# Small products inside an FFN stream: pair 5's outputs in two parts, pair 6's first products later, the last pair's outputs in two parts

## The chip, the cores and the metric

The kernel runs on one core of one Trainium2 chip. The time is device microseconds (us) of one execution; medians are over several executions. The span in a profile is of one execution, from its first to its last instruction, and is about 1.7 us shorter than the time of the same execution (337.6 against 335.9 us for the kernel before). A change counts as faster or slower when the 95% interval of the ratio of times is clear of 2%, as the same when it lies within 2%, and as unclear when it holds the 2% line.

## The reference, cut to what matters

```
scores = scale * q @ k^T                    # 8 batches, 8 heads, 576 positions, 64 per head
ret    = (scores * Dmat) @ v                # Dmat[i, j] = gamma_h ** (i - j) for i >= j, else 0
x      = ret as (4608 tokens, 512)
a, b   = x @ w_a, x @ w_b                   # 512 -> 1536 each
out    = (a * b) @ w_out                    # 1536 -> 512, fp32
```

The kernel computes the first half by blocks: 18 pairs of 128-token blocks, with a running state (a 64 x 64 sum of k^T v per head) carried from block to block. The FFN takes 512 tokens (two pairs) at a time, in two of the ten blocks 256.

## The kernel before

TensorE gets one long stream of FFN products (`pa`, `pb`, `po`; 512 columns each, 256 in `pa` and `pb` of the two short blocks). The small products of the pairs are put between them, in "stretches". A stretch takes one pair out (its outputs `o`) and another in (its `kv` and its scores `sc`):

```python
    def stretch(into, outof):
        flush()                                   # work left for VectorE and ScalarE
        ...
        if outof is not None:
            o = ps_o[0].tile([128, 2, HP, 2, 64], FP32, tag="o", name="o2")
            begun = Begun()
            from_states(outof, o, begun)          # 32 small matmuls: outputs from states
            kp = int(0 in (block_of(outof, 0), block_of(outof, 1)))
            nc.scalar.copy(fence, o[:, :, 0, kp, 0])      # the "fence"
        if into is not None:
            convert, convert_swapped = keyed(into, outof is None)   # 32: kv
            masked = matched(into)                                  # 32: scores
        if outof is not None:
            scaled = from_keys(outof, o, begun)   # 32: outputs from keys, onto the same o
            later.append(lambda: scaled(0))
            later.append(lambda: scaled(1))
        ...
```

Both halves of the outputs add into the same PSUM tile, from different quarters of the array. The fence, a tiny ScalarE copy that reads the tile, makes the second half wait until the first is written. With `kv` and `sc` between them that wait is hidden.

Where a stretch goes is set by a list of positions, counted in FFN units (one unit is a product of 512 columns). Block 2 (256 tokens) covers units 216 to 288, of which 264 to 288 are its `po`; block 3 begins at 288 and needs the outputs of pairs 4 and 5.

```python
    todo += [(170, stretch, (3, None)), (197, stretch, (4, 3)),
             (232, stretch, (5, 4)), (266, stretch, (6, 5)),
             (372, stretch, (7, 6)), (408, stretch, (8, 7))]
    ...                                           # later pairs; the last is (None, 17)
    casts = {3: 104, 4: 104.1, 5: 141, 6: 200, 7: 250, 8: 330}
    turns = {4: 104.2, 5: 145, 6: 210, 7: 338, 8: 345}
    loads = {7: 212, 8: 271, 9: 345.1, 10: 345.2}
```

`casts` are GpSimd's conversions of q, k (`qkb`) and of v with its decay (`vb`); `turns` are two DMA transposes of `qkb` per pair, giving `qkT`; `loads` bring in q, k, v. Transposes, loads and stores share one DMA queue, issued in order by SyncE (SP).

## Time and profile before

| | kernel before |
|---|---|
| time, median (lowest to highest) | 337.17 us (335.87 to 337.80, 4 runs) |
| span of the profiled run | 335.9 us |
| TensorE busy | 322.2 us, 96% (3611 matmul records of 3648) |
| TensorE idle in the stretch (6 in, 5 out) | 2.23 + 1.27 us |
| mean granted clock, whole span | 0.988 |

Of the 13.7 us in which TensorE is not busy, part lies at the start and the end of the program (the first and the last slice are at 8 and 6 tenths), and part is no idle time at all: this trace lacks 37 matmul records, and a lacking record reads as idle time ended by "issue" (often a bracket of 0.16 us). The rest is what a change of order can win. The prediction below shows the lines: read the busy rows first, then the row of the granted clock, then who waited for whom. In a timeline line the first number is the start, the second the length, and the bracket the idle time before it with what ended it.

### The profile page before, as it was taken

Reading aid. Unit: us, or ns where it says so; the run is one execution under the profiler, and the core shown is the slowest. Engines: PE = TensorE matmul, PEld = TensorE weight load, DVE = VectorE, ACT = ScalarE, POOL = GpSimd, SP = SyncE. Lnnn points to the kernel's source line nnn. Section 1 sums busy time; section 2 is a strip of 40 time slices with the busy share of each in tenths; the row PEclk is TensorE's granted clock in tenths of the full one; section 3 lists DMA queues with packets and bytes.
Section 4 is the critical chain, followed back from the end, with each engine's and each line's share of the span. In section 5 each row is a group of like instructions: output and inputs, shape, how many; then the busy total and the mean of one; then the engine's idle time right before and its main releaser. Section 6 shows DMA issues by size and latency. Waiting matters only on the chain.

```text
span 335.9 us, 8671 instructions
## 1 busy us (share of the span) xinstructions
PE 322.2 (96%) x3611; PEld 169.4 (50%) x3648; DVE 162.1 (48%) x290; ACT 129.2 (38%) x277; POOL 114.6 (34%) x146
## 2 busy tenths in 40 slices
PE   8999999999599998999999999999999999999996
PEld 4644457868444454545454545454445444444443
DVE  5744445666433366565356535653465346413321
ACT  7725743554243343252335233523332433213321
POOL 3960178721558276446033703470340000000000
PEclk9999999999779999999999999999999999999999
DMA  7999999999699997994499448964860320031013
GB/s 207 252 189 204 265 224 221 172 219 216 108 204 254 217 209 189 217 208 73 130 213 209 79 125 182 213 113 122 180 139 4 119 70 0 2 94 33 1 23 102
DMA packets 143175, 50.37 MB, mean 150 GB/s; under 512 B 124576, under 2 KB 138656, under 8 KB 143136
## 3 DMA queue, kind: packets, MB, share of 16 engines
q1 hardware_dynamic: 138384, 45.10, 65.0%
q0 software_dynamic: 4752, 4.72, 8.7%
q8 instruction: 28, 0.46, 0.6%
q14 instruction: 11, 0.09, 0.1%
HBM read 37.75 MB, written 9.44 MB: 140 GB/s over the span
## 4 chain that ended last, share of the span: by engine, by line
PE 93%; issue 2%; DMA 1%; DVE 1%; POOL 1%; ACT 1%; ACTq 0%; DVEq 0%; POOLq 0%
PE po L716 28%; PE pb L697 27%; PE pa L682 26%; PE w L740 2%; PE o L602 2%; PE o L589 1%; PE sc L563 1%; DMA qkT<-qkb 1%; PE kv L359 1%; PE kv L506 1%; PE tp L316 1%; PE sc L331 1%; POOL qkb L444 1%; PE o L409 1%; PE pa L664 0%
## 5 line engine op out<-in xcount | busy, mean ns | idle before, releaser
L702 DVE TENSOR_TENSOR hT<-ha,pb 128x512 bf16<-128x512 bf16 (+1 forms) x120 | 75.7, 633 | 103.3 <-PE pb L697 98.1
L697 PE MATMUL pb<-xT,wb_sb 128*128 128x512 bf16 (+1 forms) x473 | 111.5, 357 | 0.5
L690 ACT CAST ha<-pa 128x512 bf16<-128x512 f32 (+1 forms) x120 | 64.7, 542 | 119.6 <-PE pa L682 118.4
L682 PE MATMUL pa<-xT,wa_sb 128*128 128x512 bf16 (+1 forms) x459 | 108.4, 357 | 1.4 <-issue 1.0
L716 PE MATMUL po<-wo_sb,hT 128*128 128x512 bf16 (+1 forms) x430 | 96.6, 378 | 2.7 <-issue 2.5
L697 PEld LDWEIGHTS <-wb_sb 128*128 128x128 bf16 x480 | 46.8, 98 | 46.4 <-issue 0.3
L682 PEld LDWEIGHTS <-wa_sb 128*128 128x128 bf16 x474 | 45.5, 98 | 45.1 <-issue 0.2
L716 PEld LDWEIGHTS <-hT 128*128 128x128 bf16 x444 | 42.7, 99 | 49.0 <-issue 3.2
L440 POOL CAST qkb<-qf 64x1024 bf16<-64x1024 f32 x15 | 15.4, 1029 | 87.0 <-DMA qf<-in_q_dram 76.9
L445 POOL TENSOR_TENSOR vb<-vf,vs 128x1024 bf16<-128x1024 f32 x15 | 28.5, 1901 | 15.0 <-PE o L602 5.4
L725 ACT COPY osb<-po 128x512 f32<-128x512 f32 (+1 forms) x21 | 12.1, 575 | 53.0 <-PE po L716 50.0
L727 DVE COPY osb<-po 128x512 f32<-128x512 f32 (+1 forms) x16 | 10.8, 674 | 40.6 <-PE po L716 40.6
L526 DVE TENSOR_TENSOR sums<-kv,sums 128x256 f32<-128x256 f32 x46 | 19.5, 423 | 2.8 <-PE kv L506 0.8
L612 DVE TENSOR_TENSOR xT<-o,qs 128x512 bf16<-128x512 f32 x30 | 19.5, 682 | 2.8 <-PE o L602 2.8
L572 DVE TENSOR_TENSOR sT<-sc,mask 128x512 bf16<-128x512 f32 x30 | 19.5, 679 | 0.0
L444 POOL CAST qkb<-kf 64x512 bf16<-64x512 f32 x30 | 17.6, 614 | 0.9
L444 POOL CAST qkb<-qf 64x512 bf16<-64x512 f32 x30 | 17.6, 614 | 0.6
L440 POOL CAST qkb<-kf 64x1024 bf16<-64x1024 f32 x15 | 15.5, 1033 | 5.3 <-DMA kf<-in_k_dram 4.8
L530 ACT CAST states<-sums 64x512 bf16<-64x512 f32 x26 | 16.0, 617 | 0.3
L740 PE MATMUL w<-ones 128*128 128x256 bf16 (+1 forms) x36 | 8.6, 370 | 1.5 <-DVE ones L197 1.5
L299 POOL CAST qkb<-kf 128x512 bf16<-128x512 f32 x5 | 3.1, 614 | 19.0 <-DMA kf<-in_k_dram 19.0
L631 ACT COPY fence<-o 128x2 f32<-128x2 f32 x15 | 2.4, 160 | 16.6 <-PE o L589 16.6
(81 smaller groups left out, 161.7 us busy)
## 6 DMA issues: line engine op xcount, KB each, us to landing
qf<-in_q_dram SPq DMA_DIRECT2D x32, 256.0 KB, 4.2
kf<-in_k_dram SPq DMA_DIRECT2D x32, 256.0 KB, 4.8
vf<-in_v_dram SPq DMA_DIRECT2D x32, 256.0 KB, 5.2
out_dram<-osb SPq DMA_DIRECT2D x25, 256.0 KB, 2.2
out_dram<-osb SPq DMA_DIRECT2D x22, 128.0 KB, 2.5
wo_sb<-in_moe_w_out_dram POOLq DMA_DIRECT2D x3, 512.0 KB, 16.8
qf<-in_q_dram SPq DMA_DIRECT2D x8, 128.0 KB, 3.3
kf<-in_k_dram SPq DMA_DIRECT2D x8, 128.0 KB, 3.4
```

The costliest lines, as they stand in the source:

```text
L440: nc.gpsimd.tensor_copy(qkb[0:64, w], t[0:64])
L444: nc.gpsimd.tensor_copy(to[:, :, 1 - r], fro[:, :, r])
L445: nc.gpsimd.tensor_tensor(vb.rearrange("p (k h d) -> p k h d", k=2, h=H), vf.rearrange("p (k h d) -> p k h d", k=2, h=H), vs2[:, 2 if n in ...
L526: nc.vector.tensor_tensor(sums[:, i], own, prev, op=ALU.add)
L530: nc.scalar.copy(to(half(1 - r)), fro(half(r)))
L572: nc.vector.tensor_tensor(sT[:, on].rearrange("p c k s -> p (c k) s"), sc[:, on].rearrange("p c k s -> p (c k) s"), mask3.unsqueeze(1).to_ ...
L612: nc.vector.tensor_tensor(x_of(t0, 128).rearrange("p c (a s) -> p c a s", a=2), o[:, :, :, kp].rearrange("p a c s -> p c a s"), qs[:, :, s ...
L682: nc.tensor.matmul(pa[:, 0:n], wa_sb[:, c, fs], xT[:, c], start=(c == 0), stop=(c == NC - 1))
L690: nc.scalar.copy(ha[:, 0:n], pa[:, 0:n])
L697: nc.tensor.matmul(pb[:, 0:n], wb_sb[:, c, fs], xT[:, c], start=(c == 0), stop=(c == NC - 1))
L702: nc.vector.tensor_tensor(hT[:, F, 0:n], has[F][:, 0:n], pb[:, 0:n], op=ALU.mult)
L716: nc.tensor.matmul(po[:, 0:width], hT[:, F, u * 128:(u + 1) * 128], wo_sb[:, F, cols], start=(F == 0), stop=(F == NF - 1))
```

## The change

Its intent: pair 6 is not ready when pair 5's outputs are due, so take the two apart. Pair 5's outputs are issued in two parts with four FFN products between, which also cover the fence; pair 6's first products go into block 3; and its transposes go behind pair 7's loads in the DMA queue. The last pair's outputs are also issued in two parts.

```diff
+    def open_outputs(n):
+        o = ps_o[0].tile([128, 2, HP, 2, 64], FP32, tag="o", name="o2")
+        begun = Begun()
+        from_states(n, o, begun)
+        kp = int(0 in (block_of(n, 0), block_of(n, 1)))
+        nc.scalar.copy(fence, o[:, :, 0, kp, 0])
+        opened[n] = o, begun
+    def close_outputs(n):
+        scaled = from_keys(n, *opened.pop(n))
+        later.append(lambda: scaled(0))
+        later.append(lambda: scaled(1))
+    def open_alone(n):
+        flush()
+        open_outputs(n)
 ...                                       # stretch() now uses these
-             (232, stretch, (5, 4)), (266, stretch, (6, 5)),
+             (232, stretch, (5, 4)), (266, open_alone, (5,)),
+             (270, close_outputs, (5,)), (312, stretch, (6, None)),
 ...
-                 (starts[n] - 44, stretch,
-                  (n + 2 if n + 2 < NP else None, n + 1))]
+                 (starts[n] - 44, stretch, (n + 2, n + 1))
+                 if n + 2 < NP else
+                 (starts[n] - 44, open_alone, (n + 1,))]
+    todo += [(starts[NP - 2] - 40, close_outputs, (NP - 1,))]
 ...
-    turns = {4: 104.2, 5: 145, 6: 210, 7: 338, 8: 345}
+    turns = {4: 104.2, 5: 145, 6: 240, 7: 338, 8: 345}
```

More of the change, by code (lines that the diff above doesn't have):

```diff
@@ L618, in from_keys @@
         return scaled
+    opened = {}
+    def open_outputs(n):
[12 more added lines that the diff above has]
+        open_outputs(n)
     def stretch(into, outof):
@@ L625, in stretch @@
         if outof is not None:
-            o = ps_o[0].tile([128, 2, HP, 2, 64], FP32, tag="o", name="o2")
-            begun = Begun()
-            from_states(outof, o, begun)
-            kp = int(0 in (block_of(outof, 0), block_of(outof, 1)))
-            nc.scalar.copy(fence, o[:, :, 0, kp, 0])
-        if into is not None:
-            convert, convert_swapped = keyed(into, outof is None)
-            masked = matched(into)
-        if outof is not None:
-            scaled = from_keys(outof, o, begun)
-            later.append(lambda: scaled(0))
-            later.append(lambda: scaled(1))
-        if into is not None:
-            later.append(lambda: (convert(), masked(0)))
-            later.append(lambda: (convert_swapped(), masked(1)))
+            open_outputs(outof)
+        convert, convert_swapped = keyed(into, outof is None)
+        masked = matched(into)
+        if outof is not None:
+            close_outputs(outof)
+        later.append(lambda: (convert(), masked(0)))
+        later.append(lambda: (convert_swapped(), masked(1)))
     WCOLS = [3, 4, 5]
```

## The prediction

> **What bounds the kernel now.** I read the page from the top: busy shares, then slices, then the list of waits, then the chain and the TensorE timeline where the slices dip.
>
> ```profile
> PE 322.2 (96%) x3611; PEld 169.4 (50%) x3648; DVE 162.1 (48%) x290; ACT 129.2 (38%) x277; POOL 114.6 (34%) x146
> ...
> PE   8999999999599998999999999999999999999996
> ...
> PEclk9999999999779999999999999999999999999999
> DMA  7999999999699997994499448964860320031013
> ```
>
> TensorE (PE) is the bound nearly everywhere. So only two things can change the time: what TensorE executes, which the change leaves alone (the instruction orders of the two kernels have the same 7298 TensorE rows), and the places where it stands still or runs at a lower clock. A slice is 335.9/40 = 8.4 us. There is one bad place after the start: slice 11 (84.0 to 92.4 us) has PE at 5, and slices 11 and 12 have the granted clock at 7. The list of waits names it:
>
> ```profile
> ACT fence L631 <- PE o L589: 16.6, 15, 2.5
> ...
> PE kv L506 <- POOL vb L445: 2.2, 1, 2.2
> ...
> PE sc L563 <- DMA qkT<-qkb: 1.3, 1, 1.3
> ...
> PE o L602 <- ACT fence L631: 0.3, 1, 0.3
> ```
>
> Three waits of TensorE, each happening once. The first two lie in the stretch that is changed first (pair 6 in, pair 5 out), the third in the one changed last (pair 17 out alone). Timeline of TensorE (start, length, what, idle before it):
>
> ```profile
> 85.51 1.02 PE L716 MATMUL po<-wo_sb,hT 128*128 128x512 bf16 x3
> 86.46 0.44 PE L589 MATMUL o<-qkT,states 64*64 64x64 bf16 x32
> 89.14 0.64 PE L506 MATMUL kv<-vb,qkb 64*64 64x64 bf16 x32 [2.23 <-POOL vb L445]
> 91.05 0.64 PE L563 MATMUL sc<-qkT 64*64 64x64 bf16 x32 [1.27 <-DMA qkT<-qkb]
> 91.50 0.62 PE L602 MATMUL o<-sT,vb 64*64 64x64 bf16 x32
> 92.46 5.89 PE L716 MATMUL po<-wo_sb,hT 128*128 128x512 bf16 x19 [0.33 <-issue]
> ```
>
> The stretch issues four groups of 32 small matmuls: pair 5's outputs from states (L589), pair 6's kv and scores (L506, L563), pair 5's outputs from keys (L602). Pair 6 is not ready, and as the order is fixed, pair 5's second half and the FFN products behind it wait too. The FFN products after it run at half pace. Both show in the windows (start:end, length, busy of five engines, granted clock, DMA share, GB/s), the first line being an undisturbed stretch (5 in, 4 out):
>
> ```profile
> 76.50:77.80 1.30, 1.30 (x123) 1.20 (x121) 0.42 (x1) 0.27 (x2) 0.00 (x0) 1.00 1.29 274
> ...
> 86.40:92.50 6.10, 2.26 (x130) 1.97 (x131) 1.95 (x5) 0.16 (x1) 2.61 (x3) 0.71 0.86 134
> 92.40:98.40 6.00, 5.94 (x21) 2.38 (x20) 2.33 (x4) 2.55 (x6) 2.60 (x4) 0.72 1.05 200
> ```
>
> Why pair 6 is late: its q lands at 82.54 us (GpSimd's cast starts there), GpSimd needs until 87.12 for the q and k casts and 89.09 for vb, and the second DMA transpose, issued at 87.14, lands 3.87 us later, at 91.01. Nothing of that chain waits for TensorE.
>
> **What the Trainium skill says.** (1) "TensorE: Matmul & The Clock Gate", Part 1: the array has a half-rate and a full-rate clock, falls back after about 3.4 us of idleness and needs about as long to recover; 512-column products start 426.7 ns apart cold and 215.7 warm. The trace agrees: the first weight loads of L716 after the bubble start at 92.46, 92.89, 93.31, 93.74 (0.427 apart), and warm FFN groups of four take 0.86 (0.216 each). (2) "TensorEngine Tiling (Array Packing)", Tiling Modes, Key Properties: changing the tiling mode drains TensorE. The trace shows a small sum: the weight load of the first small group has 0.42 us of idle time each time, and the stretch as a whole costs more than its matmuls (below). (3) "DMA: Bandwidth & Descriptors", Queues, rings and completion order: on each DMA engine descriptors are consumed in ring order. That fits q, k, v of a pair landing in the order issued, and bears on a rival below.
>
> **The change, part by part.**
>
> Part 1, cost of the stretch now. The last FFN slot before it starts at 86.16 (85.51 plus three spacings of 0.216; one record of four is missing), so FFN would continue at 86.37. The first product after it has no record either; one cold spacing before 92.46 gives 92.03. Delay: 92.03 - 86.37 = 5.66 us. The 20 output products left in the block then need until 98.18 (next pa), 6.15 us against 20 x 0.216 = 4.31: 1.84 us for the cold clock. Sum 7.50 us beyond plain FFN work.
>
> Part 2, cost of the same 128 matmuls when all is ready. A clean stretch later: last po slot before it ends its spacing at 256.94, groups start at 257.04, 257.31, 257.57, 257.89, and FFN resumes at 258.30 (258.51 less one unrecorded product). That is 1.36 us: about 0.28 per group of 32, and 0.10 at entry plus some 0.13 at exit, so about 0.23 for one change of mode.
>
> Part 3, after. Pair 5's first half: 0.23 + 0.28 = 0.51. Four FFN products (no cost; they had to run anyway, and cover the fence, whose ACT copy takes 0.16). Second half: 0.51. Pair 6's kv and scores, 24 FFN units into block 3: 0.23 + 2 x 0.28 = 0.79. Sum 1.81 us, with two more changes of mode than now. Gain if nothing waits: 7.50 - 1.81 = 5.7 us.
>
> Part 4, the last pair. Now: the FFN would go on at 290.64 and does at 291.83 (292.05 less one missing record), 1.19 us, of which the small groups start at 290.73 and 291.45. These are 0.72 apart where 0.27 is normal, so the fence stops TensorE for 0.45, not the 0.3 in the list. After: two blocks of 0.51 = 1.02. Gain about 0.2 us, as the second change of mode eats half.
>
> Part 5, moved DMA. The transposes of pair 6 go from position 210 to 240, so in the DMA queue's order they now stand behind six loads of pair 7 and a store. Pair 6's kv also goes to the output banks in place of two FFN banks; no FFN product waits for a bank in the trace, so I give this 0.
>
> Does pair 6 become ready in time? TensorE reaches it at: 86.37 + 0.51 + 0.86 + 0.51 + 16 x 0.216 (= 91.7, start of block 3) + 24 x 0.216 = 96.9 us; the scores, which need the transposes, 0.4 later, at 97.2. Values (vb) are ready at 89.1: fine. The transposes: loads of pair 7 start issuing at 82.9 (now 89.63), when the queue is free after the store; their 1.57 MB follow v of pair 6, whose transfer now ends at about 84.2 (DMA goes idle there). At the 220 GB/s of a busy stretch, 7.1 us: 91.4. The store, 0.26 MB: 92.6. Two transposes of about 1.8 us DMA time each: 96.2, and some 0.5 to 1 us until the semaphore: 96.7 to 97.2, an estimate from these numbers. Needed at 97.2. That is a tie; I take 0.3 us of expected wait, 1.5 at worst.
>
> Sum: 5.7 + 0.2 - 0.3 = 5.6 us; 337.5 - 5.6 = 331.9 us, 1.7% less.
>
> **The rivals.** (a) The wait moves with the transposes: the queue's order makes pair 6's scores wait at about 97 us for 1 to 2 us. For it: the tie above. Against: pair 7's loads use time in which the DMA engines idle now (84.2 to 86.1). Gain 4 to 5 us, time 332.5 to 333.5. (b) Hidden anyway: the 5.7 us come back as waits further on, since all later pairs come 5.6 us sooner for TensorE while transfers do not. For it: DMA shares of 9 until slice 20. Against: pair 7's loads come sooner as well, and no later stretch shows a wait on DMA; pair 7's vb ends at 102.25 and its stretch is at 117.3, 15 us of room. Then 335 to 338. (c) The cold clock stays: one small wait near 97 plus three mode changes could bring the clock down again. Against: the clean stretches run at 1.00. It would cost up to 1.8 us: about 333.5. (d) More is gained: the median of 337.5 carries more cold time than I count. Time 330 to 331; the spread of the kernel before, 335.87 to 337.8, allows for it.
>
> **Range and chances.** The line for 2% is 330.7 us, a gain of 6.75. The full gain without any wait is 5.9, so crossing the line needs about 0.9 us of luck or of (d): 0.15. Losing 2% would need a new wait of over 12 us: 0.01. The range from 330.2 to 334.3 holds (a), (c) and half of (d), but not (b).
>
> **What would show it.** Right: no TensorE wait on vb L445 or fence; PEclk of 9 in slices 11 and 12; the three blocks of small groups near 86.5, 87.8 and 97 us costing 0.5, 0.5 and 0.8; FFN products at 0.216 between; the last pair's halves about 1.4 us apart with no fence wait; span near 330.2. Block 3's first product moves from 98.2 to about 91.7 us and the last pair saves 0.2. Wrong: a TensorE wait on qkT<-qkb over 1 us near 97 (a); clock under 1 between 92 and 100 (c); new waits on vb, qkT or xT between 105 and 140 us (b).

## The result, and the profile after

| | before | after |
|---|---|---|
| time, median (lowest to highest) | 337.17 us (335.87 to 337.80) | 331.52 us (331.00 to 332.27) |
| runs | 4 | 4 |
| span of the profiled run | 335.9 us | 329.3 us |
| TensorE busy | 322.2 us, 96% | 323.7 us, 98% |
| matmul records, of 3648 | 3611 | 3648 |
| mean granted clock | 0.988 | 1.00 |

The ratio is 0.9839 (95% interval 0.9802 to 0.9876). A ratio is the mean time of one kernel's fast runs over that of the other's in the same rounds, so it is not quite the ratio of the medians. By the 2% rule this is "the same", and 1.6% less.

In the changed file the FFN lines stand 13 lower (`po` is L729, `pa` L695, `pb` L710) and the fence is L629. The page after, the rows of TensorE, of the granted clock and of the DMA engines in 40 slices of 8.2 us:

```profile
PE   8999999999999999999999999999999999999996
...
PEclk9999999999999999999999999999999999999999
DMA  7999999989999999993799158935840510031013
```

The dip in slice 11 and the two slices of lower clock are gone. In the list of waits (total, times, longest) only one line of TensorE's matmuls is left, at the start of the program:

```profile
PE w L753 <- DVE ones L197: 1.5, 1, 1.5
```

The timeline of TensorE after, where the bubble was:

```profile
85.42 1.02 PE L729 MATMUL po<-wo_sb,hT 128*128 128x512 bf16 x4
86.38 0.45 PE L589 MATMUL o<-qkT,states 64*64 64x64 bf16 x32
86.75 1.04 PE L729 MATMUL po<-wo_sb,hT 128*128 128x512 bf16 x4
87.72 0.45 PE L602 MATMUL o<-sT,vb 64*64 64x64 bf16 x32
88.10 3.63 PE L729 MATMUL po<-wo_sb,hT 128*128 128x512 bf16 x16
91.56 1.03 PE L695 MATMUL pa<-xT,wa_sb 128*128 128x512 bf16 x4
...
96.83 0.45 PE L506 MATMUL kv<-vb,qkb 64*64 64x64 bf16 x32
97.11 0.44 PE L563 MATMUL sc<-qkT 64*64 64x64 bf16 x32
97.48 1.04 PE L695 MATMUL pa<-xT,wa_sb 128*128 128x512 bf16 x4
```

There is no bracket in any of these lines (this trace lacks no matmul record, so brackets of 0.16 us with "issue" are gone for that reason alone). Each part of pair 5's outputs delays the FFN by little: four `po` from 85.42 would be followed by the next at 86.28, and it starts at 86.75 (0.47 us); the second part costs 88.10 - 87.61 = 0.49; pair 6's two groups 97.48 - 96.74 = 0.74. Block 3 starts at 91.56 in place of 98.18 us. The same two windows that were at 0.71 and 0.72 of the clock before (columns as there):

```profile
86.40:92.50 6.10, 6.10 (x90) 3.00 (x90) 1.29 (x2) 1.33 (x3) 5.92 (x7) 1.00 1.11 211
92.40:98.40 6.00, 6.00 (x90) 2.92 (x89) 2.73 (x5) 1.75 (x3) 3.34 (x4) 1.00 1.02 204
```

TensorE is busy throughout, at full clock. The last pair, timeline before:

```profile
289.77 1.03 PE L716 MATMUL po<-wo_sb,hT 128*128 128x512 bf16 x4
...
290.73 0.45 PE L589 MATMUL o<-qkT,left_states 64*64 64x64 bf16 x32
...
291.45 0.45 PE L602 MATMUL o<-sT,vb 64*64 64x64 bf16 x32 [0.28 <-ACT fence L631]
...
292.05 1.24 PE L716 MATMUL po<-wo_sb,hT 128*128 128x512 bf16 x5 [0.16 <-issue]
```

and after:

```profile
283.42 1.03 PE L729 MATMUL po<-wo_sb,hT 128*128 128x512 bf16 x4
284.38 0.45 PE L589 MATMUL o<-qkT,left_states 64*64 64x64 bf16 x32
284.75 1.04 PE L729 MATMUL po<-wo_sb,hT 128*128 128x512 bf16 x4
285.72 0.44 PE L602 MATMUL o<-sT,vb 64*64 64x64 bf16 x32
286.10 4.28 PE L729 MATMUL po<-wo_sb,hT 128*128 128x512 bf16 x19
```

The fence wait is gone, and a second visit of the small groups has come. Delay 0.47 + 0.49 = 0.96 us against 1.19.

One more difference was not looked for. In the stretch (8 in, 7 out) FFN products resume later in the profile before than after, both with all inputs ready. Before, then after:

```profile
125.51 0.45 PE L589 MATMUL o<-qkT,states 64*64 64x64 bf16 x32
...
127.73 2.11 PE L716 MATMUL po<-wo_sb,hT 128*128 128x512 bf16 x9 [0.89 <-issue]
```

```profile
119.64 0.45 PE L589 MATMUL o<-qkT,states 64*64 64x64 bf16 x32
...
121.15 5.35 PE L729 MATMUL po<-wo_sb,hT 128*128 128x512 bf16 x24
```

From the first small group to the first `po` it is 2.00 us before (127.73 less one unrecorded product of 0.22) and 1.51 after. "Issue" means that the profile shows nothing waited for.

The two spans differ by 6.6 us, and four pieces add up to it, all read as differences between the two timelines: 0.09 until block 2's `po` (85.51 and 85.42); 5.79 from there to the stretch (7 in, 6 out) (117.27 - 85.51 = 31.76 against 111.39 - 85.42 = 25.97); 0.49 in the stretch (8 in, 7 out); 0.23 in the last pair. The medians differ by 5.65.

### The profile page after: what moved, and what is told of

It is laid out like the page before. It is cut to its first block, busy times and chain, and to the rows that moved or that the text cites. A ratio compares the mean times of both kernels' runs of the same rounds, so it can differ in the third digit from the quotient of the medians.

```text
span 329.3 us, 8714 instructions
## 1 busy us (share of the span) xinstructions
PE 323.7 (98%) x3648; PEld 168.1 (51%) x3648; DVE 162.1 (49%) x290; ACT 129.0 (39%) x277; POOL 114.5 (35%) x146
## 4 chain that ended last, share of the span: by engine, by line
PE 95%; DMA 2%; DVE 1%; SPq 0%; ACT 0%; issue 0%; POOL 0%; ACTq 0%; DVEq 0%; POOLq 0%
PE po L729 29%; PE pb L710 28%; PE pa L695 28%; PE o L589 2%; PE o L602 2%; DMA qf<-in_q_dram 2%; PE sc L563 1%; PE kv L506 1%; PE kv L359 1%; PE tp L316 1%; PE sc L331 1%; PE o L409 1%; PE w L753 0%; PE pa L677 0%; SPq L153 0%
## 5 line engine op out<-in xcount | busy, mean ns | idle before, releaser
L710 PE MATMUL pb<-xT,wb_sb 128*128 128x512 bf16 (+1 forms) x480 | 111.8, 358 | 0.1
L695 PE MATMUL pa<-xT,wa_sb 128*128 128x512 bf16 (+1 forms) x474 | 110.3, 358 | 0.0
L729 PE MATMUL po<-wo_sb,hT 128*128 128x512 bf16 (+1 forms) x444 | 97.8, 374 | 0.0
L710 PEld LDWEIGHTS <-wb_sb 128*128 128x128 bf16 x480 | 46.8, 98 | 46.4 <-issue 0.3
L695 PEld LDWEIGHTS <-wa_sb 128*128 128x128 bf16 x474 | 45.5, 98 | 44.9 <-issue 0.2
L729 PEld LDWEIGHTS <-hT 128*128 128x128 bf16 x444 | 42.1, 98 | 46.8 <-issue 0.3
L629 ACT COPY fence<-o 128x2 f32<-128x2 f32 x15 | 2.4, 160 | 16.6 <-PE o L589 16.6
```

What stands on the lines that cost most here:

```text
L695: nc.tensor.matmul(pa[:, 0:n], wa_sb[:, c, fs], xT[:, c], start=(c == 0), stop=(c == NC - 1))
L710: nc.tensor.matmul(pb[:, 0:n], wb_sb[:, c, fs], xT[:, c], start=(c == 0), stop=(c == NC - 1))
L729: nc.tensor.matmul(po[:, 0:width], hT[:, F, u * 128:(u + 1) * 128], wo_sb[:, F, cols], start=(F == 0), stop=(F == NF - 1))
```

## The experiments

All outputs are right. Theory: the whole gain is pair 6 no longer holding up TensorE, made of idle time and of a cold clock behind it; the splits save only a fence stall. Rivals: the splits bring it; the DMA queue's new order brings it; the cold clock is chance. The first four ran on one chip (kernel before: median 338.12 us, 7 runs), the next four on a second (337.08, 7 runs), three on a third (338.34, 11 runs) and the last on a fourth (337.29, 11 runs).

### Last pair alone

The kernel before with the last pair's outputs in two parts, which is the changed kernel with

```diff
-             (232, stretch, (5, 4)), (266, open_alone, (5,)),
-             (270, close_outputs, (5,)), (312, stretch, (6, None)),
+             (232, stretch, (5, 4)), (266, stretch, (6, 5)),
-    turns = {4: 104.2, 5: 145, 6: 240, 7: 338, 8: 345}
+    turns = {4: 104.2, 5: 145, 6: 210, 7: 338, 8: 345}
```

> The kernel before with only the last pair's outputs in two parts. My theory: worth about 0.2 us (two blocks of about 0.48 us for one of 1.19 us with a fence stall of 0.45), so within noise of the kernel before, about 337.0 us, the bubble of pair 6 and the cold clock still there. Rival: splitting the outputs round FFN products is what brings the gain, then this run alone is over 1 us faster than before.

Measured: 336.50 us, ratio 0.9978 (0.9912 to 1.0043): no clear difference. The bubble was there (2.29 and 1.35 us), with a clock of 0.994 in the profiled run and 0.990 to 0.994 in the four. The interval excludes the gain of the change (0.984), so this split alone does not bring it. It does not exclude the rival's 1 us; against that stands the trace, in which the bubble is unchanged. The lower median goes with a milder fall of the clock (0.993 or 0.994 in three of its four runs, 0.993 to 0.995 in three of seven of the kernel before; see the last experiment).

### All but the last pair's split

```diff
+    def whole(n):
+        open_alone(n)
+        close_outputs(n)
-                 (starts[n] - 44, open_alone, (n + 1,))]
-    todo += [(starts[NP - 2] - 40, close_outputs, (NP - 1,))]
+                 (starts[n] - 44, whole, (n + 1,))]
```

> The changed kernel with the last pair's outputs in one piece again. My theory: 0.2 us slower than the changed kernel (about 331.7 us), fence stall of 0.45 us back in the trace, clock 1.00. Rival: over 0.5 us slower.

Measured: 331.38 us, ratio 0.9814. The times do not resolve 0.2 us. The trace does: the fence stall is back (small groups at 284.34 and 285.06), and the delay of the last pair is 285.67 less one unrecorded product, 285.45, less the due start 284.25: 1.20 us against 0.96.

### The move without pair 5's split

```diff
-             (266, open_alone, (5,)), (270, close_outputs, (5,)), (312, stretch, (6, None)),
+             (266, whole, (5,)), (312, stretch, (6, None)),
```

(`whole` as in the run above; the last pair stays in two parts.)

> Pair 6 moved into block 3, its transposes late in the queue, but pair 5's outputs in one piece, without FFN products between (last pair split as in the changed kernel). My theory: the move brings everything, the split saves only the fence stall of 0.45 less one change of mode of about 0.2: 331.7 to 331.9 us, and the trace shows one block of about 1.2 us at 86.4. Rival (the split of pair 5 matters): over 1 us slower than the changed kernel, 332.5 us or more.

Measured: 331.79 us, ratio 0.9823 (0.9774 to 0.9873). TensorE's timeline:

```profile
86.72 0.45 PE L589 MATMUL o<-qkT,states 64*64 64x64 bf16 x32
87.44 0.45 PE L602 MATMUL o<-sT,vb 64*64 64x64 bf16 x32 [0.27 <-ACT fence L629]
88.04 4.26 PE L733 MATMUL po<-wo_sb,hT 128*128 128x512 bf16 x19 [0.16 <-issue]
```

The delay of pair 5's outputs is 1.20 us (from 86.62, when the next `po` was due, to 87.82), against 0.96 in two parts. So pair 5's split is worth 0.24 us and the move nearly all.

### The split without the move

Pair 5 in two parts, pair 6 kept early behind them:

```diff
-             (270, close_outputs, (5,)), (312, stretch, (6, None)),
+             (270, close_outputs, (5,)), (274, stretch, (6, None)),
-    turns = {4: 104.2, 5: 145, 6: 240, 7: 338, 8: 345}
+    turns = {4: 104.2, 5: 145, 6: 210, 7: 338, 8: 345}
```

> Pair 5 split, but pair 6's products kept early, four FFN products behind pair 5's second part, transposes early in the queue as before. My theory: TensorE arrives at 89.0, waits about 0.3 us for vb and about 1.7 us for the transposes (landing near 91.2): about 2 us slower than the changed kernel if the clock stays full (333.5 us), up to 3.8 us slower if the clock falls (335.3 us). Rival (the split brings the gain, as it lets FFN products and outputs go ahead): within 0.5 us of the changed kernel.

Measured: 333.41 us, ratio 0.9869 (0.9818 to 0.9920), clock 0.999 to 1.00. TensorE's timeline:

```profile
90.98 0.45 PE L506 MATMUL kv<-vb,qkb 64*64 64x64 bf16 x32 [0.86 <-POOL vb L445]
92.54 0.45 PE L563 MATMUL sc<-qkT 64*64 64x64 bf16 x32 [1.11 <-DMA qkT<-qkb]
93.14 2.54 PE L729 MATMUL po<-wo_sb,hT 128*128 128x512 bf16 x11 [0.16 <-issue]
```

Both waits are back, 1.97 us in all, shorter because pair 5's second part and eight FFN products now stand ahead of them. This fits the medians of the same rounds: 333.41 us is 1.6 to 2.0 us above the two kernels with pair 6 moved (331.79 and 331.38), which themselves lack a split worth 0.24 us by their traces. And the clock stayed full: the small groups take 0.45 as usual.

### The transposes' place in the queue

```diff
-    turns = {4: 104.2, 5: 145, 6: 240, 7: 338, 8: 345}
+    turns = {4: 104.2, 5: 145, 6: 210, 7: 338, 8: 345}
```

> The changed kernel, but pair 6's transposes stay at their early place in the DMA queue, ahead of pair 7's loads. My theory: the transposes land near 91 us in place of about 96.8, TensorE asks at 97.1, so both are in time and pair 7 has 15 us of room: no change, within 0.3 us of the changed kernel. Rival (the queue's order is part of the gain, as blocked loads of pair 7 come late): a new wait between 105 and 125 us, 1 us or more slower.

Measured: 331.74 us, ratio 0.9836 (0.9802 to 0.9870). No wait near 97 us, and none where the rival placed it, but one of 0.61 us at 134.5, for pair 9's transposes:

```profile
134.49 0.45 PE L563 MATMUL sc<-qkT 64*64 64x64 bf16 x32 [0.61 <-DMA qkT<-qkb]
```

To tell a rule from chance, the same kernel ran again, as the last of the twelve:

> The kernel with pair 6's transposes early in the queue once more. Its first profile showed no wait near 97 us, but one of 0.61 us at 134.5 us for the transposes of pair 9, which were issued about 1.3 us later than in the changed kernel. If that comes from the queue standing still behind pair 6's transposes (84 to 86 us), it comes again in this profile: a wait of 0.2 to 1.2 us at about 134.5, DMA issues from 98 us on 1 us or more later than in the changed kernel, time 0.2 to 0.6 us above it. If the first was chance, no wait there.

Measured: 331.75 us (330.67 to 333.13, 6 runs), ratio 0.9835 (0.9802 to 0.9867). The expected wait did not come: no wait of TensorE on `qkT`, and a span of 329.0 us, shorter than the 329.3 of the changed kernel. What did come again is its supposed cause (24 GB/s from 85 to 87 us in the first profile). Windows from 84 to 86 us (last two columns: DMA share and GB/s), this kernel and then the changed one:

```profile
84.00:86.00 2.00, 2.00 (x17) 1.38 (x15) 1.62 (x5) 1.54 (x4) 1.94 (x3) 1.00 0.19 45
```

```profile
84.00:86.00 2.00, 2.00 (x17) 1.46 (x15) 1.62 (x5) 1.63 (x4) 1.94 (x3) 1.00 0.91 209
```

With the transposes early, the queue waits behind them for GpSimd's casts and moves little (45 against 209 GB/s), and pair 9's transposes are issued at 127.86 rather than 126.81 us. The changed kernel's second profile has 127.82 too, but with a later TensorE. What counts is the time from the second transpose's issue to the due start of pair 9's scores: 5.66 and 4.98 us in the two profiles of the changed kernel, 4.14 here, and 3.4 in the profile with the wait. So one profile shows a short wait and the other none. The queue's new order fills the hole, but its worth, if any, is below what these times resolve.

### Pair 6 earlier by steps

The changed kernel with the position of pair 6's products at 304, 296 and 286 (done at unit 288) in place of 312, for instance

```diff
-             (270, close_outputs, (5,)), (312, stretch, (6, None)),
+             (270, close_outputs, (5,)), (304, stretch, (6, None)),
```

> The changed kernel with pair 6's first products 8 FFN units (1.7 us) sooner. TensorE then asks for the scores at 95.4 us, the transposes land at about 96.75: wait of 1.3 us. My theory: so short a wait leaves the clock full, and the cost is the wait alone: span 1.3 us longer than that of the changed kernel (329.3). Rival (any wait here brings the clock down): 1.3 plus about 1.8 us.

> The same, 16 FFN units (3.45 us) sooner: asks at 93.65, wait of about 3.1 us. My theory: near the idle time at which the clock falls (3.5 us in two pieces did it in the kernel before): span 3.1 us longer if the clock stays, about 5 us if it falls. Rival (the cold clock was chance): 3.1 and clock 1.00.

> The same, at the border of blocks 2 and 3, 24 FFN units (5.2 us) sooner: asks at 91.9, wait of about 4.85 us. My theory: the clock falls, as idle time and cold time add: span 4.85 plus 1.8 to 2.5 us longer, 336 or so, granted clock under 1 in the window behind. Rival (the cold clock was chance): 4.85 longer, clock 1.00.

Measured: 331.96, 335.14 and 339.29 us (two runs each), mean clocks in the profiled runs 1.00, 0.994 and 0.99. The last is 0.5% slower than the kernel before, in the same rounds. Windows from 98.4 to 104.0 us, the first of the kernel at 304, the second of that at 286:

```profile
98.40:104.00 5.60, 5.60 (x27) 2.53 (x26) 3.60 (x6) 3.35 (x7) 3.31 (x5) 1.00 0.94 221
```

```profile
98.40:104.00 5.60, 5.60 (x18) 2.03 (x17) 1.30 (x3) 1.17 (x2) 3.15 (x4) 0.60 1.25 239
```

TensorE reads as busy in both, but it got through 27 matmul records in one and 18 in the other. The busy row does not show a cold clock; the clock column does.

The table parts wait from cold clock. The wait is measured from start to start: the start of a delayed group less its due start (0.28 us behind the group before it, from the prediction's clean stretch). The cold cost is the time from `kv` to the first L589 of the stretch (7 in, 6 out), less 0.2158 us per FFN unit between (the chain has 24 in 5.18 us), less 0.74 for the two groups and their mode change, less the wait. Where pair 6 comes in block 2, the count starts when FFN would resume, 0.40 behind the start of the last small group.

| kernel | wait, us | in | cold cost, us |
|---|---|---|---|
| pair 6 at 304 | 0.73 | one piece | 0.03 |
| split without the move | 2.21 | two pieces | 0.0 |
| pair 6 at 296 | 3.16 | one | 1.72 |
| pair 6 at 296, again (below) | 3.28 | one | 1.71 |
| last pair alone | 3.97 | two | 1.65 |
| kernel before | 4.03 | two | 1.97 |
| pair 6 at 286 | 5.05 | one | 2.89 |

Two working examples: for 296, `kv` starts at 94.43, `sc` at 97.87 (due 94.71: wait 3.16) and the stretch (7 in, 6 out) at 117.31, 22.88 us after `kv`; 80 units are 17.26, so 22.88 - 17.26 - 0.74 - 3.16 = 1.72. For the kernel before, `kv` came 2.40 and `sc` 1.63 late; FFN would resume at 91.50 + 0.40 = 91.90, 108 units and 0.1 for entry end at 115.3, and the stretch came at 117.27.

So in these profiles waits up to 2.2 us (the longest in two pieces) cost their length, and waits of 3.2 us and more cost some 1.7 to 2.9 us on top. The expectation for 304 was too pessimistic in the wait (1.3 expected, 0.73 measured): the transposes landed by 96.09, not 96.75.

### The same kernel again, the step at 296, and a try at a better one

The changed kernel unaltered, then with the stretch (5 in, 4 out) four units later, then the step at 296 as above:

```diff
-             (232, stretch, (5, 4)), (266, open_alone, (5,)),
+             (236, stretch, (5, 4)), (266, open_alone, (5,)),
```

> The changed kernel once more, unaltered, as the yardstick of this chip for the next two. Expected 331.5 us, clock 0.999 to 1.00 in every run, ratio to the kernel before 0.984.

> A try at a better version: the stretch of pairs 5 in and 4 out goes 4 FFN units (0.87 us) later, since in two profiles of earlier experiments it waited 0.62 and 1.09 us for pair 5's transposes and in the others not at all. If such waits make up the spread of the changed kernel (331.0 to 332.3), the median falls by 0.2 to 0.4 us and the slow runs go. Rival: pair 5's states, made by VectorE and ScalarE after this stretch, then come too late for its outputs at 86.4 us, and a new wait of about 0.5 us eats it: same time.

> The kernel with a wait of about 3.0 us at 94.9 us again, for more runs of it: the two so far took 336.68 us at a mean clock of 0.994 and 333.60 at 0.999. My theory: 3 us lies at the edge where the clock may fall or not[...]; so the runs fall into two groups, about 333.5 with a clock of 0.999 to 1.00 and 335.5 to 336.5 with about 0.994. Rival (time is set by the length of the wait alone): one group, with clock and time unrelated.

Measured: the changed kernel 331.59 us, ratio 0.9813 (0.9778 to 0.9848), clock 1.00 in all six runs. The later stretch 331.56 us (330.40 to 332.84), ratio 0.9805: no better, with the same spread, and the profile of its slowest run shows no wait of TensorE on `qkT`; so waits for pair 5's transposes are not what spreads the runs. I have no version that beats the changed kernel.

The step at 296: 337.79 us, ratio 0.9998 (0.9953 to 1.0043), as slow as the kernel before. The expectation failed in its first group: none of the six runs kept its clock. They had 0.994 or 0.995 (336.33, 336.47, 337.94 us) or 0.988 to 0.990 (337.65, 339.75, 340.81 us). With the two runs on the other chip, one of eight, at 0.999, came through (333.60 us). So 3 us brings the clock down nearly always, by two different amounts. The kernel before has the same two: of its 36 runs beside the experiments, 11 had a clock of 0.993 to 0.995 (median 336.86 us) and 25 one of 0.988 to 0.990 (median 338.32 us).

The clock column over short windows shows what the two amounts are. In every profile with a lowered clock it was at half for 3.41 us ("last pair alone", both at 296) or for 6.83 us (kernel before, 286), so for one or two steps of 3.41 us. Three steps of the kernel before, then the only cold step of "last pair alone" (after the length, the first number is TensorE's busy time; the third from the end is the clock):

```profile
85.49:88.91 3.42, 1.36 (x36) 0.64 (x36) 0.75 (x2) 0.39 (x2) 3.28 (x4) 1.00 0.70 109
88.91:92.32 3.41, 1.71 (x96) 1.57 (x97) 1.77 (x5) 0.00 (x0) 0.18 (x1) 0.50 0.88 139
92.32:95.73 3.41, 3.27 (x8) 1.22 (x8) 2.41 (x4) 0.04 (x1) 1.19 (x2) 0.50 1.23 233
```

```profile
91.89:95.30 3.41, 3.41 (x9) 1.22 (x9) 2.42 (x4) 0.27 (x1) 0.87 (x1) 0.50 1.29 241
```

In these five profiles the step that ended with the clock's fall held 2.0 to 3.4 us of idle time of TensorE (2.06 in the first line; 2.22 in "last pair alone", 2.47 and 2.02 at 296, 3.41 at 286), and the steps before it at most 1.64 us. Where the step after the fall held 1.70 (second line) or 1.16 us more (286), a second cold step followed; where TensorE was busy throughout it, the clock came back. Half of a step is 1.71 us, close to the cold cost of the three profiles with one (1.65 to 1.72). So what counts is how much of a wait falls into one step; that the one run at 296 with a clock of 0.999 had its wait divided between two steps would fit, but it left no trace.

## Why the prediction was right

Predicted 331.9 us (330.2 to 334.3), measured 331.52. The closeness, 0.4 us, is partly luck: the base of 337.5 came from three runs of a kernel whose medians ran from 337.08 to 338.34 us in later rounds, and the gain in medians is 5.65 us in the first measurement and 6.75 in the repeat. By its own steps:

- **Part 1, the cost of the stretch now (7.50 us).** Shown. With pair 6 out of the way, block 2's `po` to the stretch (7 in, 6 out) got 5.79 us shorter. "Last pair alone", which keeps the bubble, keeps the time. (The list of waits puts the 10.1 us of GpSimd before pair 6's q cast, at 82.54, down to TensorE. The profile after puts 11.17 us down to the load of q, with the cast at 82.83; so the prediction's reading, that q had just landed, is the likelier.)
- **The cold clock (1.84 us of it).** Shown as an effect of the wait: the two profiles with waits of 0.73 and 2.21 us kept the clock and the five with 3.16 to 5.05 us lost it (table), and the changed kernel runs at 1.00. The prediction's "the trace agrees" holds for the spacing of the products, 0.427 and 0.216 us, and not for the idle time: the clock fell at 88.91 us, 2.0 us after the last small matmul (86.90). And the weight loads that it names are not the first after the bubble, which are at 92.05 and 92.07; the spacing stands. The size by the table's reckoning is 1.97, as it counts the slow small groups too.
- **Parts 2 and 3, what remains (1.81 us).** Measured 0.47 + 0.49 + 0.74 = 1.70. A visit of small groups costs about 0.21 us for the change of mode (0.47 less the 0.26 that a second group adds, 0.74 - 0.48), not 0.23.
- **Part 4, the last pair (0.2 us).** 0.23 in the trace, 0.24 when undone; the times alone cannot show it. The estimate that the fence stalls TensorE 0.45 us rather than the listed 0.3 held, and the same was found for pair 5.
- **Part 5, the tie.** No wait in the changed kernel, so the 0.3 us set aside was not needed, but the tie was real: TensorE asked at 97.11, and with the step at 304 the transposes, issued 0.65 us earlier than in the changed kernel (91.35 against 92.00), landed at 96.09. By that, an estimate, they land near 96.7 in the changed kernel: some 0.4 us of room. (Its trace has 3.4 us from issue to landing, and the second issue at 93.46: near 96.8.)
- **Not in the sum:** the 0.49 us in the stretch (8 in, 7 out), and 0.09 at the start. I claim no cause. The profiled spans differ by more than the medians because the profiled run of the kernel before (337.6 us) lies above its median and that of the changed kernel (331.0) below.

Of the rivals, (a) did not come and "the split without the move" shows what it would have cost; (b) fell, as no new wait appeared behind in the changed kernel (pair 9's transposes come nearest to one); (c) fell, three mode changes left the clock full; (d), more than 6.75 us, came close: the ratio was 0.9839 in the first measurement and 0.9813 in the repeat, where the kernel before ran slower (338.34 us); the medians there differ by 6.75.

Most of the change's text is not where its gain is. The move of pair 6 by 44 units (from 268, where 266 takes effect, to 312) brings all but about half a microsecond; the two splits bring 0.24 each by the traces; the transposes' move brings nothing measurable.

## What to carry to other kernels

When one engine is the bound and takes its work in a fixed order, look for the group whose inputs come late and move that group alone, behind work that is ready; eight FFN products were not enough (2 us of wait left), 44 were. Count the price of a wait of TensorE as its length plus a cold clock once it comes to about 3 us (here 2.0 us of idle time within one 3.41 us step of the clock were enough, 1.64 were not), and read that from the clock column, since the busy row stays full. Splitting a group to hide a short stall pays only what the stall exceeds the extra change of mode by: here 0.45 less 0.21 us.

## What the Trainium skill lacked or had wrong

- "TensorE: Matmul & The Clock Gate", Part 1, has the clock fall after at least one idle window of about 3.4 us (its closing table of advice says gaps over about 3 us). Here less was enough: 2.02 to 2.47 us of idle time within one step of 3.41 us, in four profiles; 1.64 us within one step were not, nor were two pieces of 0.86 and 1.11 us. The page gives no share of a window that is enough.
- The same section gives the ramp's penalty as under 1% of a kernel. For one bubble inside a kernel it was 1.7 to 2.9 us, about 0.5 to 0.9% of 337 us: within that, but over a quarter of this change's gain. The same kernel lost one or two steps (mean clocks of 0.994 and 0.989), which fits the free-running window that the section describes; it draws from that window how the warm-up scatters, and not that the price of a wait does.
- "TensorEngine Tiling (Array Packing)", Tiling Modes, says that changing the mode drains TensorE but gives no time. Here one visit of 64 x 64 groups between 128 x 128 products cost 0.21 us beyond the groups.
- No page that I read explains the 0.3 to 0.9 us that TensorE stood still in the stretch (8 in, 7 out) in several profiles (0.89 before, 0.60 with the last pair alone, 0.69 with the move alone) with nothing waited for in the records.
